# Scaling only one half of the query features, with a new hand-kept order of all operations

## The chip, the cores and the metric

The kernel runs on one core of a Trainium2 chip. The metric is the time on the device in microseconds (us), the median of several runs; the profile is of one execution. TensorE (PE in the profile) multiplies matrices, VectorE (DVE), ScalarE (ACT) and GpSimd (POOL) work element by element, and SyncE (SP) issues transfers. Every engine takes its own instructions strictly in order and waits for the others by semaphores.

## The reference

Two layers, each a linear attention followed by a gated feed-forward part, with a residual around both. There are 2048 tokens of 512 numbers, 32 heads of 16, and a feed-forward width of 1376.

```python
pq = einsum("bhsd,hdf->bhsf", q, w_phi);  pk = the same of k
phi_q = concat([softmax(pq), softmax(-pq)], -1);  phi_k = the same of pk
kv = einsum("bhsf,bhsd->bhfd", phi_k, v);  z = sum of phi_k over the tokens
o = (phi_q @ kv) / (phi_q @ z + 1e-6);  attention = o @ wo
# feed-forward: gate = x @ W_gate; h = relu(gate) * (x @ W_up); h @ W_down
x = x + attention(layernorm(x)); x = x + feed_forward(layernorm(x))   # twice
```

Both layers use the same weights. A softmax runs over the 16 numbers of one head.

## The kernel before, in words

The tokens are 16 tiles of 128 rows, kept in `X`. `fold` multiplies w_phi into the query and key weights once at the start, so that one projection gives `pq` or `pk` of a tile: w_phi is spread to block-diagonal form (`Wblk`, line 409), the weight blocks are transposed (`wT`) and multiplied with it (line 448), and copied to `Wk2` and `Wq2` (operations named `W2`). For the key weights the transposition is on TensorE (line 440), for the query weights by a transposing load on SP (line 435).

For every tile of a layer, `norm_A` computes the normalisation (statistics at line 477 and 478 on VectorE, logarithm and root at 485 and 487 on ScalarE, scaling at 495 on VectorE) and a transposition `xnTA`, by TensorE (line 466) for the first tiles, else by SP. `Keys` then does the key projection (line 535), exp(p) and exp(-p) (538, ScalarE) into the two halves of `ek`, the value projection (541) with its copy `vext` (425 on ScalarE or 426 on VectorE), the 64 sums over 16 numbers (546, VectorE), their reciprocal by logarithm and exponential (555, 558, ScalarE), two 512-wide multiplications by it (`halves`, line 509, VectorE or GpSimd), and the product with the values, summed up over all tiles (570). When all 16 tiles of a layer are in, `build` makes `R` of it (582, 587).

`query` does the same for queries: projection at 597, exponentials at 600, sums `sq` at 603, logarithm and exponential at 606 and 608, the two wide multiplications (line 509 again, named `phq`), and a transposition `fq` by SP (611). `attend` multiplies `fq` with `R` (622), divides (629 to 636), transposes (`oT`) and projects with wo (645), and adds to `X` (649). `mlp` centres (665), transposes (`xnTB`), squares (671 or 673), computes gate and up (722, and 698 for the last 96 columns), the product `hT` (726 to 739), and the down projection (762) with its sum into `X` (769). Feed-forward blocks are of 1, 1, 2, 4, 4, 2, 2 tiles in the first layer and 1, 1, 2, 4, 4, 2, 1, 1 in the second. The first gate matmul of the first block needs the whole of `R`, and so the keys and values of all 16 tiles.

Nothing is scheduled at run time. The 1880 operations are made in a fixed list, and four constants say the rest: `ORDER` is the order in which they are emitted (so also the order on each engine), `PLACE` has a digit for each operation that has two engines to choose from (1 takes the second), `SLOTS` names the buffer that each takes, and `IDLE` counts filler matmuls on zeros ahead of each of the first TensorE operations; eight more (`warm`, line 419) run while the first loads are under way. The four constants were computed beforehand by a planner with a model of the engines' costs; the costs at each `op(...)` are its inputs and have no effect on the chip.

Of the kernel before, what the change touches and what calls it, by code (L numbers as in the profile page):

```python
# [8 lines left out]
P = 128  # L9
D = 512  # L10
H = 32
DH = 16
F = 1376
NB = D // P
# [4 lines left out]
HB = 8  # L19
NG = 2 * NB  # L20
# [92 lines left out]
def dve(n, rate=1, more=66):  # L113
    t = n / rate / 0.96 + more
    return t, t + 98
# [27 lines left out]
class K:  # L143
# [9 lines left out]
    "0101110100000000001100000100110001000011010001111000000011001101010101001001001000101001111111011010"  # L153
    "1011110000000100000001001101000000000111011001011111010111000101001100000101111101001100001101010100"
    "1111111110101010010001000011000100000000101100101010100001001100011100010000110011001101000110111001"
    "010110010110111001110100110100000"
)
SLOTS = (
    "0001425210034050000151131234202310332121143404550125d3104c02302b3020a12113g533004002394131703202e141"
    "5i022124504f013k03583226105214413624335a011h100b033c05053623122j214910170400020501131002000245011020"  # L160
    "2500001142021002010100203200101143020002012105002004314023104g13300215112012320410311e34110200400450"
    "10205113120513d5100i42221240121321402422031200151030231042100142131004133610104f33242541002510104203"
    "51101520500512052130201550414201515300804024k2232c4020121152143124212004023502a533344112050010024104"
    "02024213011055002220j4203h05133317362b222f1506242i013a114023391638231c343e352k221d014g10011500020514"
    "0010124302000012011021450000121302100024010021050012201000011011521101530431102000005112025421011101"
    "0213125200125020013101050032154203115143114220221100253415210511200211401013403005210402213013222420"
    "500210300512431510432512113015114024105320310110512400202"
)
IDLE = (
    0, 0, 0, 0, 0, 0, 0, 0, 0, 0, 2, 0, 4, 0, 0, 0, 0, 0, 0, 0, 0,  # L170
# [108 lines left out]
def kernel(  # L279
# [11 lines left out]
    def new(name, shape, dt=BF16):  # L291
        return sb.tile([P] + shape, dt, name=name)
# [586 lines left out]
```

## Time and profile before

| | |
|---|---|
| median of three runs | 377.24 us (377.06 to 377.68) |
| profiled execution, span from first to last instruction | 375.3 us |
| TensorE busy | 364.6 us, 97% |
| VectorE, ScalarE, GpSimd busy | 285.1, 209.7, 93.5 us |
| granted TensorE clock | 1.000 |

The page gives no other time of the profiled execution than its span; the median lies 1.9 us above it. Busy times count an instruction from its start to its end; matmuls are pipelined, so a row of four that follow each other every 0.216 us is shown as 1.03 us long. In the lines of the profile a PE, DVE, ACT or POOL stands ahead of the line of the code, the operation, what it writes and reads, and how many instructions were merged.

### The profile page before, as it was taken

To read this page: it belongs to the slowest core of one execution; us is meant where nothing else is said; L and a number is where in the kernel's file an instruction comes from. 1 tells how busy PE (TensorE), PEld (TensorE's weight loads), DVE (VectorE), ACT (ScalarE), POOL (GpSimd) and SP (SyncE) were. 2 spreads that over 40 slices of the span, in tenths; PEclk is the share of its full clock that TensorE was granted. 3 is DMA by queue.
4 is the path that set the end of the run, shared out by engine and by line. 5 is a ranking of instruction groups with operands and counts; after the bars stand their busy time and mean duration, and the time that the engine had idled before them with its cause. 6 is when DMAs were issued, how large, how long until landed. Compare 5 with 4: busy or idle time off the path is not lost.

```text
span 375.3 us, 7459 instructions
## 1 busy us (share of the span) xinstructions
PE 364.6 (97%) x2793; PEld 216.6 (58%) x2833; DVE 285.1 (76%) x596; ACT 209.7 (56%) x553; POOL 93.5 (25%) x91
## 2 busy tenths in 40 slices
PE   8989997999999999999999999999999999999996
PEld 4534454868554554466476555587745444558585
DVE  6999999999998673685767999999994755543322
ACT  6989999746464532265155499973425323414031
POOL 0377984341010102001004269774000000000000
PEclk9999999999999999999999999999999999999999
DMA  8858844769814221012020102968664120211110
GB/s 256 191 139 175 312 58 85 123 113 132 164 36 84 47 53 31 11 25 56 9 56 2 29 2 57 141 93 142 143 132 85 31 56 2 56 29 51 42 51 30
DMA packets 93444, 31.21 MB, mean 83 GB/s; under 512 B 85248, under 2 KB 92384, under 8 KB 93408
## 3 DMA queue, kind: packets, MB, share of 16 engines
q1 hardware_dynamic: 92992, 30.34, 39.5%
q8 instruction: 22, 0.36, 0.4%
q10 hardware_dynamic: 416, 0.39, 0.3%
q14 instruction: 14, 0.11, 0.1%
HBM read 7.91 MB, written 2.10 MB: 27 GB/s over the span
## 4 chain that ended last, share of the span: by engine, by line
PE 90%; ACT 6%; DVE 1%; POOL 1%; issue 1%; DVEq 0%; another core or an unknown queue 0%
PE b L722 37%; PE b L762 20%; PE b L645 7%; PE b L541 6%; PE b L535 6%; PE b L597 6%; PE b L698 3%; PE q L622 2%; PE q L570 2%; ACT ek L600 1%; POOL ek L509 1%; ACT ek L538 1%; PE q L419 1%; DVE sq L603 1%; ACT hT L425 1%
## 5 line engine op out<-in xcount | busy, mean ns | idle before, releaser
L722 PE MATMUL b<-xnTB,wgu 128*128 128x128 bf16 (+2 forms) x1200 | 149.6, 279 | 0.0
L722 PEld LDWEIGHTS <-wgu 128*128 128x128 bf16 x1200 | 97.1, 98 | 43.6
L509 POOL TENSOR_TENSOR ek<-ek,sk 128x512 bf16<-128x512 bf16 x47 | 51.0, 1109 | 135.5 <-ACT sk L558 108.2
L726 ACT ACTIVATE gu<-b 128x512 bf16<-128x512 f32 (+1 forms) x83 | 47.8, 580 | 64.9 <-PE b L722 64.6
L762 PE MATMUL b<-wd,hT 128*128 128x512 bf16 (+2 forms) x350 | 81.3, 372 | 0.7
L762 PEld LDWEIGHTS <-hT 128*128 128x128 bf16 (+1 forms) x363 | 34.6, 98 | 35.9 <-DVE hT L739 0.2
L509 POOL TENSOR_TENSOR ek<-ek,sq 128x512 bf16<-128x512 bf16 x38 | 42.0, 1127 | 32.6 <-ACT sq L608 18.0
L739 DVE TENSOR_TENSOR hT<-gu,b 128x512 bf16<-128x512 bf16 (+1 forms) x44 | 29.6, 676 | 18.5 <-PE b L722 16.9
L546 DVE TENSOR_REDUCE sk<-ek 128x64 f32<-128x1024 bf16 x32 | 38.7, 1210 | 5.3 <-ACT ek L538 5.2
L538 ACT ACTIVATE ek<-b 128x512 bf16<-128x512 f32 x64 | 35.9, 598 | 9.2 <-PE b L535 8.0
L603 DVE TENSOR_REDUCE sq<-ek 128x64 f32<-128x1024 bf16 x32 | 38.2, 1207 | 0.3 <-POOL ek L509 0.3
L600 ACT ACTIVATE ek<-b 128x512 bf16<-128x512 f32 x64 | 36.1, 623 | 0.6 <-PE b L597 0.5
L730 DVE TENSOR_TENSOR hT<-gu 128x512 bf16<-128x512 bf16 (+1 forms) x39 | 16.7, 429 | 22.5 <-ACT gu L741 22.3
L769 DVE SCALAR_TENSOR_TENSOR X<-b,rsB,X 128x512 bf16<-128x512 f32 (+1 forms) x33 | 23.2, 726 | 13.5 <-PE b L762 13.4
L645 PE MATMUL b<-wo,oT 128*128 128x512 bf16 x118 | 31.2, 379 | 1.2 <-ACT oT L425 0.7
L535 PE MATMUL b<-Wk,xnTA 128*128 128x512 bf16 x122 | 31.4, 379 | 0.3
L541 PE MATMUL b<-wv,xnTA 128*128 128x512 bf16 x124 | 31.0, 379 | 0.4 <-ACT xnTA L425 0.2
L597 PE MATMUL b<-Wq,xnTA 128*128 128x512 bf16 x121 | 30.5, 379 | 0.3
L741 ACT CAST gu<-b 128x512 bf16<-128x512 f32 (+1 forms) x39 | 21.7, 558 | 15.0 <-PE b L722 14.6
L649 DVE SCALAR_TENSOR_TENSOR X<-b,X 128x512 bf16<-128x512 f32 x32 | 21.8, 682 | 3.5 <-PE b L645 3.4
L636 DVE TENSOR_TENSOR o<-q,rd 128x512 bf16<-128x512 f32 x32 | 21.9, 685 | 0.8 <-ACT rd L633 0.6
L477 DVE BATCH_NORM_STATS2 bstA<-X 128x6 f32<-128x512 bf16 x32 | 21.0, 681 | 1.9 <-DMA X<-in_A_x_dram 1.8
(71 smaller groups left out, 349.1 us busy)
## 6 DMA issues: line engine op xcount, KB each, us to landing
out_dram<-X SPq DMA_DIRECT2D x15, 128.0 KB, 1.7
X<-in_A_x_dram SPq DMA_DIRECT2D x6, 256.0 KB, 4.8
wgu<-in_B_W_gate_dram SPq DMA_DIRECT2D x4, 344.0 KB, 4.0
wgu<-in_B_W_up_dram SPq DMA_DIRECT2D x4, 344.0 KB, 3.6
wd<-in_B_W_down_dram SPq DMA_DIRECT2D x5, 256.0 KB, 3.6
wv<-in_A_wqkv_dram SPq DMA_DIRECT2D x2, 256.0 KB, 4.3
wo<-in_A_wo_dram SPq DMA_DIRECT2D x4, 128.0 KB, 3.2
fq<-ek SPq DMA_TRANSPOSE x32, 3.3
```

Of the source, the lines that this page charges most:

```text
L509: e.tensor_tensor(out=out().rearrange("p g s (h f) -> p (g s h) f", f=DH)[:, lo:lo + n], in0=ek.t[:].rearrange("p g s (h f) -> p (g s h) f ...
L535: k = op("PE", mm(4, 512), due, lambda: [nc.tensor.matmul(kp.t[:], lhsT=xnTA[c][:, i, b, :], rhs=Wk2[:, b, :], start=(b == 0), stop=(b == ...
L538: e = [op("ACT", act(512), due, lambda s=s: nc.scalar.activation(out=ek.t[:, :, s, :], in_=kp.t[:].rearrange("p (g e) -> p g e", e=GQ), fu ...
L541: v = op("PE", mm(4, 512), due_v, lambda: [nc.tensor.matmul(vp.t[:], lhsT=xnTA[c][:, i, b, :], rhs=wv[:, b, :], start=(b == 0), stop=(b == ...
L546: a = op("DVE", SUM16, due, lambda: nc.vector.tensor_reduce(out=sk.t[:, row, :], in_=ek.t[:].rearrange("p g s (h f) -> p (g s h) f", f=DH) ...
L597: q = op("PE", mm(4, 512), due, lambda: [nc.tensor.matmul(qp.t[:], lhsT=xnTA[c][:, i, b, :], rhs=Wq2[:, b, :], start=(b == 0), stop=(b == ...
L600: e = [op("ACT", act(512), due, lambda s=s: nc.scalar.activation(out=ek.t[:, :, s, :], in_=qp.t[:].rearrange("p (g e) -> p g e", e=GQ), fu ...
L603: a = op("DVE", SUM16, due, lambda: nc.vector.tensor_reduce(out=sq.t[:], in_=ek.t[:].rearrange("p g s (h f) -> p (g s h) f", f=DH), axis=A ...
L645: a = op("PE", mm(4, 512), due + 3, lambda j=j, yp=yp: [nc.tensor.matmul(yp.t[:], lhsT=oT.t[:, j, b, :], rhs=wo[:, b, :], start=(b == 0), ...
L722: nc.tensor.matmul(ps.t[:, q * W:(q + 1) * W].rearrange("p (i t) -> p i t", t=P), lhsT=wgu[:, s, b, g * P:(g + 1) * P], rhs=xT.t[:, 0:n, b ...
L726: nc.scalar.activation(out=gu.t[:, 0, 0:cols], in_=gp.t[:, 0:cols], func=AF.Relu)
L762: nc.tensor.matmul(yp.t[:, 0:c1 - c0], lhsT=h.t[:m, f * W + i * P:f * W + (i + 1) * P], rhs=wd[:m, f, c0:c1], start=(f == 0), stop=(f == N ...
```

## The change

For queries, numerator and denominator of the attention both carry the factor by which a row of a head's features is scaled. The change divides both halves by the sum of exp(-p): exp(-p) stays as it is, and exp(p) is multiplied by the ratio of the sum of exp(-p) to the sum of exp(p). Logarithm and exponential run over the 32 sums of exp(p) only; a new multiplication of 32 numbers makes the ratio (in the place of the first wide one of the list), and one 512-wide multiplication is left. w_phi is centred over its last index ahead of being spread, by two small instructions, which doesn't change a softmax. Keys are computed as before. The numbers in `ORDER`, `SLOTS` and `PLACE` are all new, and the count of operations stays 1880; the placement of the choices changes so:

| operation | before | after |
|---|---|---|
| query multiplications, 512 wide | 38 POOL, 26 DVE | 24 POOL, 8 DVE |
| query ratio, 32 numbers | none | 20 POOL, 12 DVE |
| key multiplications, 512 wide | 47 POOL, 17 DVE | 43 POOL, 21 DVE |
| value copies | 19 ACT, 13 DVE | 25 ACT, 7 DVE |
| folded-weight copies | 6 ACT, 2 DVE | 8 ACT |
| copies of the up projection, else a direct product | 39 ACT, 44 DVE | 36 ACT, 47 DVE |

```diff
 IDLE = (
-    0, 0, 0, 0, 0, 0, 0, 0, 0, 0, 2, 0, 4, 0, 0, 0, 0, 0, 0, 0, 0,
+    0, 0, 0, 1, 0, 0, 0, 0, 0, 0, 1, 0, 1, 0,
...
-    c_blk = op("DVE", dve(512), 20, lambda: nc.vector.tensor_tensor(
...
+    def blocks():
+        nc.vector.tensor_reduce(out=cmean[:], in_=wf[:], axis=AX.X, op=Alu.add)
+        nc.vector.scalar_tensor_tensor(out=wf[:], in0=cmean[:].unsqueeze(2).to_broadcast([P, NB, DH]),
+                                       scalar=-1.0 / DH, in1=wf[:], op0=Alu.mult, op1=Alu.add)
+        nc.vector.tensor_tensor(
+            out=Wblk[:].rearrange("p b (j f) -> p b j f", f=DH),
+            in0=wf[:].unsqueeze(2).to_broadcast([P, NB, HB, DH]),
+            in1=Mf[:].unsqueeze(1).unsqueeze(3).to_broadcast([P, NB, HB, DH]), op=Alu.mult)
...
+        pos, neg = (lambda: sq.t[:].rearrange("p (g s h) -> p g s h", s=2, h=HG)[:, :, 0, :],
+                    lambda: sq.t[:].rearrange("p (g s h) -> p g s h", s=2, h=HG)[:, :, 1, :])
         a = op("ACT", RLN[0], due, lambda: nc.scalar.activation(
-            out=sq.t[:], in_=sq.t[:], func=AF.Ln, scale=1.0), [a], (), [sq], name="lnq")
+            out=pos(), in_=pos(), func=AF.Ln, scale=1.0), [a], (), [sq], name="lnq")
         a = op("ACT", REXP[0], due, lambda: nc.scalar.activation(
-            out=sq.t[:], in_=sq.t[:], func=AF.Exp, scale=-1.0), [a], (), [sq], name="rq")
-        a = halves("phq", ek, lambda: ek.t[:], lambda lo, n: sq.t[:, lo:lo + n], PHI["POOL"], due, [a], [], [ek, sq])
+            out=pos(), in_=pos(), func=AF.Exp, scale=-1.0), [a], (), [sq], name="rq")
+
+        def ratio(e):
+            e.tensor_tensor(out=pos(), in0=pos(), in1=neg(), op=Alu.mult)
+
+        def scale(e):
+            v = ek.t[:, :, 0, :].rearrange("p g (h f) -> p g h f", f=DH)
+            e.tensor_tensor(out=v, in0=v, in1=pos().unsqueeze(3).to_broadcast([P, NG, HG, DH]), op=Alu.mult)
+        a = op("POOL", (212, 253), due, lambda: ratio(nc.gpsimd), [a], [], [ek, sq], name="rat", port=3,
+               alt=("DVE", DVE0, lambda: ratio(nc.vector), 1))
+        a = op("POOL", (1016, 1058), due, lambda: scale(nc.gpsimd), [a], [], [ek, sq], name="phq", port=3,
+               alt=("DVE", dve(512), lambda: scale(nc.vector), 1))
```

Of the new order the prediction speaks of these places (names as in the code, with the number of the tile or block; `load2` is the first half of the key weight, `load1` the second, `load3` is w_phi, `load4` and `load5` the value weight, `load0` and `load6` on the tiles of x):

```
SP before:  load2 load3 load4 load5 load6 load7 load8 load9 load10 ... load14 wT4
SP after:   load3 load2 load6 load7 load8 load9 load13 wT4 load5 load11 load4 load14 wT6
ACT before: load0 load1 tbl ln0 rstd0 wT0 wT3 wT1 wT2 W23 xnTA0 W22 W21 vext0
ACT after:  load0 tbl load1 ln0 rstd0 wT0 wT1 ln1 W20 rstd1 wT3 wT2 xnTA0 W21 W23 W22
DVE before: hr0 hr0 zero eps ones ... masks Mg stats0 aggr0 xnA0 Wblk W20 stats1
DVE after:  ones eps hr0 masks zero ones ones hr0 stats0 ones aggr0 Wblk stats1 ones aggr1 xnA0
PE before:  warm turn0 turn1 turn3 xnTA0 turn2 fold0 fold3 fold1 fold2 V0 K0 xnTA3 xnTA2 xnTA1 V3 K1
PE after:   warm turn0 turn1 fold0 turn3 turn2 xnTA0 fold1 fold3 fold2 fold4 xnTA1 K0 K1 xnTA3 V0 xnTA2
```

More of the change, by code (lines that the diff above doesn't have):

```diff
@@ L163 @@
[L163 to L167, printed above, removed]
+    "0011432021055021001401501045313321124221352412451013e0315g31303b0305c12201i012432332391030654220f321"
@@ L311 @@
     Wblk = new("Wblk", [NB, P])
+    cmean = new("cmean", [NB], F32)
     R = new("R", [NG, GE])
@@ L408 @@
     c_m = op("DVE", (230, 330), 10, masks, [c_id], name="masks")
[L409 to L412 removed]
+    def blocks():
[6 more added lines that the diff above has]
+            in1=Mf[:].unsqueeze(1).unsqueeze(3).to_broadcast([P, NB, HB, DH]), op=Alu.mult)
+    c_blk = op("DVE", (900, 1000), 20, blocks, [c_m, l_wf], name="Wblk", port=True)
     c_mg = op("DVE", DVE0, 15000, lambda: nc.vector.tensor_tensor(
```

25 lines of the change are left out of this document (13 added, 12 removed), and 183 rows, old and new, of the table ORDER.

## The prediction

> **What bounds the kernel now.** I read the page's first part and its chain of waits first, for the engine that ends last, then the busy time by windows, for the stage that has slack, then the timeline of the start and of the stage just ahead of the first feed-forward matmul.
>
> ```profile
> span 375.3 us, 7459 instructions
> ...
> PE 364.6 (97%) x2793; PEld 216.6 (58%) x2833; DVE 285.1 (76%) x596; ACT 209.7 (56%) x553; POOL 93.5 (25%) x91
> ...
> PE 90%; ACT 6%; DVE 1%; POOL 1%; issue 1%; DVEq 0%; another core or an unknown queue 0%
> ```
>
> TensorE is 90% of the chain that ended last; VectorE is far from full as an average. The averages hide the stage, so I cut the span:
>
> ```profile
> core 0: us, PE busy (x) PEld busy (x) DVE busy (x) ACT busy (x) POOL busy (x), PEclk, DMA share, GB/s
> 0.00:10.00 10.00, 8.30 (x53) 4.22 (x55) 6.27 (x24) 6.42 (x13) 0.70 (x6) 1.00 0.83 263
> 10.00:25.00 15.00, 13.11 (x100) 6.61 (x99) 14.86 (x31) 14.88 (x47) 8.30 (x8) 1.00 0.74 172
> 25.00:40.00 15.00, 14.88 (x92) 7.32 (x95) 14.93 (x27) 13.60 (x40) 11.12 (x10) 1.00 0.82 193
> 40.00:50.00 10.00, 9.89 (x80) 5.24 (x81) 9.99 (x10) 10.00 (x32) 10.00 (x11) 1.00 0.53 196
> 50.00:60.00 10.00, 9.77 (x80) 5.01 (x80) 10.00 (x15) 9.68 (x27) 6.74 (x6) 1.00 0.59 82
> 60.00:64.30 4.30, 2.59 (x33) 1.52 (x32) 4.26 (x7) 4.23 (x16) 2.12 (x2) 1.00 0.62 120
> 64.30:80.00 15.70, 15.54 (x219) 12.88 (x220) 15.70 (x35) 10.42 (x34) 5.70 (x5) 1.00 0.76 123
> ...
> 220.00:240.00 20.00, 19.84 (x155) 10.26 (x155) 19.49 (x23) 19.67 (x58) 19.83 (x19) 1.00 0.43 66
> ...
> 340.00:360.00 20.00, 19.90 (x172) 14.37 (x172) 6.06 (x11) 6.46 (x12) 0.00 (x0) 1.00 0.16 45
> ```
>
> From 64.3 us on TensorE stands idle for next to nothing: 0.16 us in the 20 at the layer boundary, where the other three engines are just as full, and 0.10 in the 20 near the end. Nothing that makes VectorE or GpSimd lighter there can shorten the span. Before 64.3 us, from 10 us on, VectorE is full (0.37 us idle in 54) and ScalarE nearly, while TensorE has holes. The first feed-forward matmul needs all keys and values, hence VectorE's sums. **So the change pays only by what it takes off the front, up to the first gate matmul:**
>
> ```profile
> 1.01 0.27 DVE L396 MEMSET zero<- 128x256 uint32 x1
> ...
> 1.34 3.60 PE L419 MATMUL q<-zero 128*128 128x512 bf16 x8 [1.34 <-DVE zero L396]
> 1.34 0.28 DVE L405 TENSOR_REDUCE Mf<-ident 128x8 f32<-128x128 bf16 x1
> ...
> 1.67 1.28 ACT L373 ACT_TABLE_LOAD   x1 [1.67 <-PEq L863]
> ...
> 4.72 0.90 PE L440 MATMUL b<-ident,hT 128*128 128x128 bf16 x12
> ...
> 5.22 2.05 ACT L425 CAST hT<-b 128x512 bf16<-128x512 f32 x4 [0.16 <-PE b L440]
> ...
> 7.19 1.87 DVE L477 BATCH_NORM_STATS2 bstA<-X 128x6 f32<-128x512 bf16 x3
> ...
> 9.18 1.03 PE L535 MATMUL b<-Wk,xnTA 128*128 128x512 bf16 x4
> ...
> 10.04 1.03 PE L419 MATMUL q<-zero 128*128 128x512 bf16 x4
> ...
> 34.04 1.89 PE L535 MATMUL b<-Wk,xnTA 128*128 128x512 bf16 x8
> ...
> 42.32 0.67 PE L570 MATMUL q<-vext,ek 128*128 128x65 bf16 x16
> ...
> 56.68 1.56 ACT L600 ACTIVATE ek<-b 128x512 bf16<-128x512 f32 x3
> ...
> 64.25 1.95 PE L722 MATMUL b<-xnTB,wgu 128*128 128x128 bf16 x32
> ```
>
> The columns are start, length, engine, line, operation and count. The first key projection runs at 9.18, the first gate matmul (call it G0) at 64.25, and everything behind G0 takes 375.3 - 64.25 = 311.0 us. The profiled execution's span is 375.3; the median of the runs is 377.24, so 1.9 us lie around the span, and I carry them along.
>
> TensorE's own need between the two marks: four 512-wide matmuls start to start in 0.863 us (a row of eight lasts 1.89, one of four 1.03), a group of eight K'V matmuls in about 0.25 (sixteen in 0.67, less the tail of 0.17), a transposition of four 128-wide ones in some 0.225 (twelve in 0.90, tail included). By the code's list the old order has, between the end of K0 at 10.04 and G0, 47 projections (40.5), 19 small groups (4.8), ten transpositions and folds (2.25) and one filler group (0.86): 48.4 us in 54.2. TensorE stalls 5.8 us there, and that is the sum the change can win from.
>
> **The change part by part.** The operation list keeps its length, so order and placement can be read number by number. Prices for the other engines, from the groups of instructions by form (count, then busy us and mean ns of one, then the idle time before them):
>
> ```profile
> L509 DVE TENSOR_TENSOR ek<-ek,sq 128x512 bf16<-128x512 bf16 x26 | 19.1, 744 | 0.0
> ...
> L509 DVE TENSOR_TENSOR ek<-ek,sk 128x512 bf16<-128x512 bf16 x17 | 11.8, 708 | 1.2 <-ACT sk L558 1.2
> ...
> L426 DVE CAST vext<-b 128x512 bf16<-128x512 f32 x13 | 8.8, 680 | 1.2 <-PE b L541 1.2
> ...
> L426 DVE CAST Wk<-b 128x512 bf16<-128x512 f32 x1 | 0.7, 692 | 0.5 <-PE b L448 0.5
> ...
> L413 DVE TENSOR_TENSOR Mg<-Mf 128x4 f32<-128x4 f32 x1 | 0.2, 161 | 0.0
> ...
> L671 ACT ACTIVATE wasteA<-X 128x512 bf16<-128x512 bf16 x21 | 13.2, 627 | 14.5 <-DVE X L649 13.2 <-issue 1.1
> ...
> L608 ACT ACTIVATE sq<-sq 128x64 f32<-128x64 f32 x32 | 8.7, 275 | 0.2
> ...
> L509 POOL TENSOR_TENSOR ek<-ek,sk 128x512 bf16<-128x512 bf16 x47 | 51.0, 1109 | 135.5 <-ACT sk L558 108.2 <-DVE ek L509 24.8 <-DVE X L769 2.4
> L509 POOL TENSOR_TENSOR ek<-ek,sq 128x512 bf16<-128x512 bf16 x38 | 42.0, 1127 | 32.6 <-ACT sq L608 18.0 <-PE b L722 6.3 <-DVE lnB L677 4.9
> ```
>
> *Query scaling.* Each of 32 query tiles had two 512-wide multiplies (38 on GpSimd, 26 on VectorE); it now has one, and one multiply of 32 numbers. The new placement puts 24 wide and 20 small ones on GpSimd, 8 and 12 on VectorE. No row shows the small one. On VectorE the nearest is the 128x4 multiply, 0.16 us; on GpSimd it lies between that and a wide one, 1.1. I take 0.16 and 0.3, near the small row, for it has a sixteenth of the elements. A query's path on GpSimd goes from two passes in turn (2.2 us) to 1.4; at the upper bound it stays at 2.2. Over the kernel GpSimd loses 18 wide passes of 1.1 (four key passes leave it too) and VectorE 14 of 0.7. Most of that lies beside a full TensorE and is worth nothing; it only hides better. What the new model could win by keeping VectorE and GpSimd out of each other's way is small: VectorE's 43 wide passes are 0.744 and 0.708 on the mean against 0.68 for its plain copies, 2.1 us in all, over the whole span. The logarithm and reciprocal handle 32 columns where they had 64; there is no row for 32, so between nothing and half of 0.275 each; I take nothing.
>
> *VectorE ahead of the first centring (line 665), by the list.* Query passes go from 4 to 1 (3 x 0.744 = 2.2), value copies from 5 to 3 (1.4), folded-weight copies from 2 to none (1.4); one key pass more (0.7), and the centring of w_phi adds two small instructions on 64 elements (0.16 each as the least; at most a 512-wide one, 0.68 each; I take 0.3 for both). Sum: -4.0; instructions in a row overlap a little (three statistics in 1.87 are 0.62 each against 0.68), so **-3.7 us**. Centring delays the block weights, but the first fold waits longer for the transposed weight on ScalarE, which covers it; uncovered it costs its 0.3.
>
> *ScalarE ahead of the evacuation that G0 waits for.* Seven exponentials of queries now come behind it (7 x 0.52, three in 1.56), as do two logarithms, two reciprocals (4 x 0.27) and one square (0.63); ahead come two folded-weight and two value copies (4 x 0.51, four in 2.05). Sum: -3.64 - 1.1 - 0.6 + 2.05 = **-3.3 us**.
>
> *The start is later.* The zeros for the eight warm-up matmuls now stand behind the mask sums on VectorE: 1.34 + 0.28 + 0.27 = 1.9, so warm-up begins some 0.6 later than at 1.34, and the first weight transposition at 5.35 instead of 4.72 (the eight take 3.38). On ScalarE the table load (1.28) now stands ahead of the second half of wk, which is therefore asked for 1.3 later; w_phi goes ahead of the first half on SP, both wv halves behind x tiles and a transposing load, so V0 moves behind K1. ScalarE starts its nine wide evacuations up to the last quarter of the folded K weight at 5.35 + 0.5 = 5.85 (the 0.5 as from 4.72 to 5.22); all four quarters are now its own. Nine times 0.51 plus two small activations (0.275 each) end at 10.99: K0 at about **11.0 instead of 9.18**. Between nothing lost and the 1.8, I take it in full.
>
> **The sum.** G0 by each engine: TensorE 11.9 plus its 48 projections, 19 small groups and eight transpositions (41.4 + 4.75 + 1.8 = 47.95): not before 59.85. VectorE: 64.25 - 3.7 + 0.3 = 60.85. ScalarE: 64.25 - 3.3 + 0.6 (its later first evacuation) = 61.55. The latest holds, and three engines that are nearly level wait for each other more; for that I add 0.7, an estimate (old TensorE stalls of 5.8, of which it still has 2.4): G0 at 62.25, 2.0 us sooner. TensorE has next to no slack behind, so the 311.0 us stay: span 373.25, **time 375.2 us**. Late next is ScalarE's queue of exponentials.
>
> **Rivals.** *The late start isn't absorbed.* If TensorE's stalls behind K0 stay at 5.8, because they come from the serial steps (exponential, sum, logarithm, scaling) and not from full queues, G0 is 11.9 + 47.95 + 5.8 = 65.65, 1.4 late: 378.6; were the late half of wk to hold the fold up 1.3 more, 379.9. It decides from 4.4 us of stalls on. For it: K0 moves back 1.8 by plain queue order. Against: VectorE is never idle from 10 us on, so less of its work must show.
>
> *New waits behind G0.* The whole order is new. A stall where TensorE now has none would eat the gain: one at the layer boundary of as much as the old front's worst (60 to 64.3: 1.7 us) gives 376.9, which is the case of no change. Against: GpSimd and VectorE have less to do there, and 11 instead of 10 of layer 1's query projections come ahead of its first attention group.
>
> *All engines overlap as their lists allow.* G0 at TensorE's 59.85: 4.4 sooner, 372.8; with ScalarE's copies moved as counted this needs its queue to be lighter than 61.55 says.
>
> *A cold array.* Between warm-up and K0 TensorE has 2.9 us of small groups and 0.65 of filler (one group each in three places, where the old order had two and four in two) for 5.65 us. The eight warm-up matmuls took 0.42 each, the later filler 0.22 (a row of four lasts 1.03 with its tail). If the array went back to the slow pace there, it would lose half of another 3.4 us: 1.7, which lifts TensorE's bound from 59.85 to 61.55, level with ScalarE's, and costs perhaps 0.7 more waiting: 375.9. By the Trainium skill, TensorE: Matmul & The Clock Gate, Part 1, the clock halves after an idle window of about 3.4 us and needs one busy window to come back, which speaks against thinning out the filler. In the trace the projections right behind the holes at 8 to 11 us still ran at 0.22 each, so it hasn't happened at holes of that size.
>
> **Chances.** Forecast and its neighbours (G0 0.8 to 3 us sooner) 0.42; the lists overlap fully 0.05; cold array, faster still 0.04; late start not absorbed 0.27; new waits behind G0 0.22, of which half about cancel the gain and half go beyond to the slow side. A measurement of this kernel tells some 0.2% (0.75 us) from no change. That gives faster 0.51, same 0.11, slower 0.38. The forecast's own range is 374.2 to 376.4; the whole range, from the full overlap's 372.8 up to the late start's worst, 379.9, leaves out larger stalls behind G0.
>
> **What would show it.** Right: K0 near 11.0, G0 between 61.5 and 63, 24 wide and 20 small multiplies of queries on GpSimd, VectorE still full from 10 to 60, and 311 us from G0 to the end. Wrong: K0 later than 12, G0 at 64.3 or behind, TensorE waits for GpSimd or VectorE of over 1 us behind G0, or a tail behind G0 that differs from 311 by more than 1 us.

## The result: 0.28% faster, about half of what was forecast

| | before | after |
|---|---|---|
| time, median of six runs | 377.54 us (377.06 to 377.70) | 376.48 us (375.87 to 376.53) |
| ratio, 95% interval | | 0.9972 [0.9963, 0.9982] |
| span of the profiled execution | 375.28 us | 374.65 us |
| first key projection K0 | 9.18 | 10.18 (forecast 11.0) |
| last group of products of keys and values ends | 55.13 | 55.40 |
| first gate matmul G0 | 64.25 | 62.74 (forecast 62.25) |
| from G0 to the end | 311.03 | 311.91 (forecast 311.0) |

In the runs of before and after the time lies 1.7 to 1.9 us above the span (in f and l, below, 2.1 to 2.2). The profiled execution of before was the fastest of its runs, so spans alone show 0.63 us of the 1.06 that the medians show; where the text below compares single points of two profiles, it compares one execution of each.

The page of after, with the parts that were shown of before (span; busy time of the engines; the chain by engine):

```profile
span 374.7 us, 7403 instructions
...
PE 363.8 (97%) x2784; PEld 216.1 (58%) x2830; DVE 275.9 (74%) x587; ACT 204.3 (55%) x561; POOL 80.4 (21%) x93
...
PE 89%; issue 1%; ACT 0%; DVE 0%; DVEq 0%
```

VectorE lost 9 us, ScalarE 5, GpSimd 13, TensorE 0.8 (three fillers fewer). Of some 28 us of work that went, 1 us came off the time. The same windows, now with the cut at the new G0:

```profile
0.00:10.00 10.00, 7.26 (x54) 3.91 (x56) 6.92 (x25) 5.58 (x13) 0.70 (x6) 1.00 0.83 239
10.00:25.00 15.00, 14.58 (x96) 7.19 (x96) 14.59 (x31) 15.00 (x45) 7.24 (x8) 1.00 0.99 216
25.00:40.00 15.00, 13.28 (x87) 6.46 (x88) 15.00 (x24) 12.82 (x40) 10.84 (x12) 1.00 0.80 180
...
50.00:60.00 10.00, 9.86 (x109) 5.71 (x110) 9.99 (x13) 9.40 (x30) 8.72 (x11) 1.00 0.49 106
60.00:62.80 2.80, 2.46 (x32) 1.42 (x31) 2.58 (x6) 2.31 (x8) 1.06 (x2) 1.00 1.08 179
62.80:80.00 17.20, 17.04 (x239) 13.68 (x239) 16.50 (x38) 12.75 (x44) 6.89 (x10) 1.00 0.82 151
220.00:240.00 20.00, 19.76 (x214) 11.55 (x216) 19.04 (x31) 14.99 (x41) 5.24 (x7) 1.00 0.08 15
```

TensorE gained from 10 to 25 us (14.58 busy instead of 13.11) and ahead of G0 (0.34 idle in 2.8 instead of 1.71 in 4.3), and lost from 25 to 40 us (13.28 instead of 14.88) while VectorE is full. These are the two places that the experiments are about.

**The place of the loss.** From the timeline of after, all engines, 26 to 32 us:

```profile
26.78 2.12 POOL L513 TENSOR_TENSOR ek<-ek,sk 128x512 bf16<-128x512 bf16 x2 [0.74 <-ACT sk L562]
26.84 2.21 DVE L499 TENSOR_SCALAR xn<-X,mvA,rsA 128x512 bf16<-128x512 bf16 x2
...
29.30 1.04 PE L539 MATMUL b<-Wk,xnTA 128*128 128x512 bf16 x4 [0.57 <-DMA xnTA<-xn]
...
29.97 0.29 ACT L489 ACTIVATE lnA<-mvA,eps 128x2 f32<-128x2 f32 x1 [2.15 <-DVE mvA L482]
...
31.38 1.02 PE L545 MATMUL b<-wv,xnTA 128*128 128x512 bf16 x4 [1.04 <-ACT ek L604]
```

Two normalisations on VectorE take 2.21 us where two others take 0.73 (30.96 us, alone). They begin 0.06 us behind two passes on GpSimd and end 0.15 us behind them: VectorE stands locked out, 1.16 and 1.14 us for an instruction of 0.41. A third one, at 20.55, took 1.13. The statistics behind them come late, ScalarE waits 2.15 us for these, and TensorE waits 0.57 and then 1.04 us. Before had none of these in its first 64 us. The Trainium skill, SBUF — State Buffer, section Who interferes with whom, says just this: such a scaling in its two-port form and a GpSimd instruction take the shared ports for the whole instruction, whoever starts first. The trace agrees, 1.16 beside 0.41 us.

**The place of the gain**, from the last products of keys and values (L570, L574) to G0. TensorE's timeline of before:

```profile
54.46 0.67 PE L570 MATMUL q<-vext,ek 128*128 128x65 bf16 x16
55.19 2.54 PE L597 MATMUL b<-Wq,xnTA 128*128 128x512 bf16 x11
57.56 0.42 PE L622 MATMUL q<-R,fq 128*128 128x68 bf16 x8
57.82 1.89 PE L597 MATMUL b<-Wq,xnTA 128*128 128x512 bf16 x8
59.88 0.40 PE L466 MATMUL b<-ident,o 128*128 128x128 bf16 x4 [0.17 <-DVE o L636]
60.95 1.04 PE L645 MATMUL b<-wo,oT 128*128 128x512 bf16 x4 [0.68 <-ACT oT L425]
...
63.18 0.40 PE L466 MATMUL b<-ident,xn 128*128 128x128 bf16 x4 [0.84 <-DVE xn L665]
```

and of after:

```profile
54.73 0.67 PE L574 MATMUL q<-vext,ek 128*128 128x65 bf16 x16
55.46 0.81 PE L601 MATMUL b<-Wq,xnTA 128*128 128x512 bf16 x3
56.30 0.42 PE L638 MATMUL q<-R,fq 128*128 128x68 bf16 x8
56.56 1.89 PE L601 MATMUL b<-Wq,xnTA 128*128 128x512 bf16 x8
58.28 0.39 PE L470 MATMUL b<-ident,o 128*128 128x128 bf16 x4
58.51 1.03 PE L601 MATMUL b<-Wq,xnTA 128*128 128x512 bf16 x4
...
60.49 1.02 PE L601 MATMUL b<-Wq,xnTA 128*128 128x512 bf16 x4
```

Before runs three query projections (11 of the 12 matmuls are recorded) ahead of the first attention group and two behind it; after runs one ahead and four behind, in the waits of the serial chain: attention group, division, transposition, output projection, residual, centring, gate. And on VectorE, between R and the first division (`o`), before has two wide query scalings, after none. From VectorE's timelines, before and then after:

```profile
57.79 1.43 DVE L509 TENSOR_TENSOR ek<-ek,sq 128x512 bf16<-128x512 bf16 x2
59.15 0.68 DVE L636 TENSOR_TENSOR o<-q,rd 128x512 bf16<-128x512 f32 x1
```

```profile
57.38 0.69 DVE L652 TENSOR_TENSOR o<-q,rd 128x512 bf16<-128x512 f32 x1
```

From the last product of keys and values to G0 it is 64.25 - 55.13 = 9.12 us before and 62.74 - 55.40 = 7.34 after: 1.78 us gained here, 0.27 lost ahead of it, 0.88 lost behind it.

### The profile page after: what moved, and what is told of

Read it like the earlier page. It is cut to its first block, busy times and chain, and to the rows that moved or that the text cites. A ratio compares the mean times of both kernels' runs of the same rounds, so it can differ in the third digit from the quotient of the medians.

```text
span 374.7 us, 7403 instructions
## 1 busy us (share of the span) xinstructions
PE 363.8 (97%) x2784; PEld 216.1 (58%) x2830; DVE 275.9 (74%) x587; ACT 204.3 (55%) x561; POOL 80.4 (21%) x93
## 4 chain that ended last, share of the span: by engine, by line
PE 89%; issue 1%; ACT 0%; DVE 0%; DVEq 0%
PE b L738 37%; PE b L778 20%; PE b L661 7%; PE b L601 6%; PE b L545 6%; PE b L539 5%; PE b L714 3%; PE q L638 2%; PE q L574 2%; PE b L470 1%; ACT ek L604 0%; DVE o L652 0%; DVE X L785 0%; DVEq L890 0%; ACT lnA L489 0%
## 5 line engine op out<-in xcount | busy, mean ns | idle before, releaser
L738 PE MATMUL b<-xnTB,wgu 128*128 128x128 bf16 (+2 forms) x1200 | 154.5, 279 | 0.2 <-ACT rd L649 0.2
L778 PE MATMUL b<-wd,hT 128*128 128x512 bf16 (+2 forms) x342 | 83.9, 372 | 0.9
L513 POOL TENSOR_TENSOR ek<-ek,sk 128x512 bf16<-128x512 bf16 x43 | 46.7, 1107 | 122.6 <-ACT sk L562 121.7
L755 DVE TENSOR_TENSOR hT<-gu,b 128x512 bf16<-128x512 bf16 (+1 forms) x47 | 30.8, 666 | 30.2 <-ACT gu L742 16.4
L604 ACT ACTIVATE ek<-b 128x512 bf16<-128x512 f32 x64 | 37.0, 606 | 6.9 <-PE b L601 6.7
L542 ACT ACTIVATE ek<-b 128x512 bf16<-128x512 f32 x64 | 36.8, 623 | 6.6 <-PE b L539 6.6
L757 ACT CAST gu<-b 128x512 bf16<-128x512 f32 (+1 forms) x36 | 20.5, 569 | 25.9 <-PE b L738 25.7
L539 PE MATMUL b<-Wk,xnTA 128*128 128x512 bf16 x122 | 32.2, 379 | 1.1 <-DMA xnTA<-xn 0.6
L545 PE MATMUL b<-wv,xnTA 128*128 128x512 bf16 x124 | 31.8, 379 | 1.3 <-ACT ek L604 1.0
L622 POOL TENSOR_TENSOR ek<-ek,sq 128x512 bf16<-128x512 bf16 x24 | 25.3, 1060 | 30.4 <-DVE rsB L701 14.3
L746 DVE TENSOR_TENSOR hT<-gu 128x512 bf16<-128x512 bf16 (+1 forms) x36 | 15.2, 424 | 10.1 <-ACT gu L757 10.0
```

The lines of the kernel that those rows point to most:

```text
L513: e.tensor_tensor(out=out().rearrange("p g s (h f) -> p (g s h) f", f=DH)[:, lo:lo + n], in0=ek.t[:].rearrange("p g s (h f) -> p (g s h) f ...
L539: k = op("PE", mm(4, 512), due, lambda: [nc.tensor.matmul(kp.t[:], lhsT=xnTA[c][:, i, b, :], rhs=Wk2[:, b, :], start=(b == 0), stop=(b == ...
L542: e = [op("ACT", act(512), due, lambda s=s: nc.scalar.activation(out=ek.t[:, :, s, :], in_=kp.t[:].rearrange("p (g e) -> p g e", e=GQ), fu ...
L545: v = op("PE", mm(4, 512), due_v, lambda: [nc.tensor.matmul(vp.t[:], lhsT=xnTA[c][:, i, b, :], rhs=wv[:, b, :], start=(b == 0), stop=(b == ...
L604: e = [op("ACT", act(512), due, lambda s=s: nc.scalar.activation(out=ek.t[:, :, s, :], in_=qp.t[:].rearrange("p (g e) -> p g e", e=GQ), fu ...
L738: nc.tensor.matmul(ps.t[:, q * W:(q + 1) * W].rearrange("p (i t) -> p i t", t=P), lhsT=wgu[:, s, b, g * P:(g + 1) * P], rhs=xT.t[:, 0:n, b ...
```

## The experiments

The theory at first was the prediction's: lighter queues on VectorE and ScalarE bring G0 forward. The rivals were that the order does it, or that locks, the start, or waits behind G0 decide the size. Ratios are to the kernel before on the same chip, five rounds each.

**Order and scaling apart.** Two kernels with one half of the change each.

```diff
 a_oldorder_newscale: code of after (scaling, centring), with before's ORDER, SLOTS and IDLE
+the ratio takes the place of a tile's first wide multiply; in 13 of layer 0's 16 tiles the wide one is on VectorE
 b_neworder_oldscale: ORDER, SLOTS and IDLE of after, with before's code of the scaling
```

> The new scaling and the centring with the old ORDER, SLOTS, PLACE and IDLE: in each query pair the first multiplication of the old order becomes the small ratio, the second the one wide scaling, on the engines that the old order gave to these places. Theory A (the front is bound by the engines' queues, the order has only to use what the scaling frees): four of the query passes ahead of the first centring are some 2 us of VectorE and now 2 small and 2 wide ones, so G0 comes 0.5 to 1.2 us sooner than at 64.25 and the time is 0.2 to 0.4% below the kernel before. Rival B (only the new order pays): no change from the kernel before, within 0.2%.

> The new ORDER, SLOTS, PLACE and IDLE with the old scaling of queries (two wide multiplications, the first in the place of the ratio) and without centring. Theory A: seven ratios ahead of the first gate matmul become wide passes of GpSimd, 0.8 us more each, but VectorE has the same work there, so G0 moves by less than 0.5 us from that of the changed kernel and the time lies between the two, 0.1 to 0.3% below the kernel before. Rival B (only the order pays): the same as the changed kernel, 0.28% below the kernel before. Rival C (the order needs the lighter GpSimd): slower than the kernel before by 0.3% or more.

| | last K'V ends | G0 | behind | median | ratio |
|---|---|---|---|---|---|
| a | 55.09 | 64.16 | 311.60 | 377.62 | 1.0013 [1.0005, 1.0022] |
| b | 57.79 | 65.49 | 318.13 | 385.25 | 1.0220 [1.0206, 1.0233] |

Neither half gains. The lighter scaling in the old order moves nothing; the new order with the old scaling loses 2.2%. The gain needs both.

**Locks.** c takes two of the three normalisations out of the way of GpSimd, h the third as well, d reads and writes every second number, in the hope that the instruction then leaves the shared ports alone.

```diff
 c_xn_first, VectorE:  -stats10 stats15 xnA6 xnA7   +xnA6 xnA7 stats10 stats15
 h_xn_all, VectorE:    c, and xnA9 directly behind xnA8
 d_step2:              -out=xn[:, j], in0=x        +out, in0 as "p (c s) -> p s c", s=2, for tiles 6, 7 and 9
```

> The changed kernel with one pair of statistics (tiles 10 and 15) moved behind the scaling of tiles 6 and 7 on VectorE, so that the scaling runs before GpSimd starts its two passes at 26.8 us. Lock theory: the scaling no longer waits out two GpSimd passes (2 x 0.73 us), TensorE's stalls at 29.3 (0.73) and 31.4 (1.21) shrink by 1 us or more, G0 comes 0.8 to 1.5 us sooner, and the time is 0.2 to 0.4% below the changed kernel. Rival (the transposing transfers on SP, queued behind weight loads, set these stalls): the scaling takes 0.41 us, the stalls stay, and the time is that of the changed kernel within 0.1%.

> The changed kernel with all three locked scalings moved ahead of GpSimd's passes: statistics of tiles 10 and 15 behind the scaling of tiles 6 and 7, and the scaling of tile 9 directly behind that of tile 8. Lock theory: no scaling in the first 64 us lasts over 0.6 us, and G0 comes another 0.2 to 0.7 us sooner than with two of them moved (61.42); time 0.2 to 0.4% below the changed kernel. Rival (the third lock is covered by other queues): G0 at 61.4 again, time as with two moved.

> The changed kernel, same order and engines; only the scaling of tiles 6, 7 and 9 of the first layer reads and writes every second element, then the rest. If that takes the instruction out of the mode in which it shares a port with GpSimd, each lasts some 0.6 to 0.65 us whatever GpSimd does, instead of 1.13 to 1.16 with a lock and 0.41 without. Lock theory: 0.5 us less in each of three places, TensorE's stalls at 29.3 and 31.4 shrink by 0.7 us or more, time 0.15 to 0.3% below the changed kernel. Rival (transfers): no change within 0.1%. Rival (the wait isn't the lock's): still over 1.1 us each.

c: G0 at 61.42, 1.32 us sooner than after; 375.71 us, 0.9963 [0.9951, 0.9975]. h: G0 61.73, 376.00 us, 0.9961 [0.9949, 0.9973], so the third lock had been covered. d: G0 63.14, 376.81 us, 0.9987 [0.9979, 0.9996]. TensorE's wait in c, and VectorE's normalisations in d:

```profile
30.06 1.02 PE L551 MATMUL b<-wv,xnTA 128*128 128x512 bf16 x4 [0.57 <-ACT ek L610]
```

```profile
20.69 1.30 DVE L500 TENSOR_SCALAR xn<-X,mvA,rsA 128x512 bf16<-128x512 bf16 x1
27.11 2.38 DVE L500 TENSOR_SCALAR xn<-X,mvA,rsA 128x512 bf16<-128x512 bf16 x2
```

In c the wait at 29.3 is gone, the other has halved, and the same value projection starts 1.32 us sooner (30.06 instead of 31.38), as G0 does: the locks cost after what the trace says, 1.3 us in its front. In time the ratios, each to before on the same chip, put it at some 0.3 us (0.9963 beside 0.9972), and their intervals overlap: what c gains over after at G0 is seen in the profile, what it gains in time is not clear of the noise. In d each of the three is still locked, so this way out fails here; the Trainium skill, VectorE: DVE Perf Modes, section What auto-detection actually checks, ties only the packed form to a step of one and not the use of both ports, and the 1.30 us agree.

**The start, and everything at once.** e brings the start back, m and g reorder more of VectorE's statistics and ScalarE's exponentials on top of c and h.

```diff
 e_start:        SP -load3 load2  +load2 load3;  VectorE: the zeros for the warm-up first
 g_all:          h and e; ScalarE: both exponentials of tile 2 ahead of ln9
 m_stats_first:  c; VectorE: stats15 stats14 aggr15 aggr14 ahead of stats10
```

> The changed kernel with the first half of the key weight asked for ahead of w_phi again, and the zeros for the warm-up matmuls ahead of the other fills on VectorE. Theory (a late start is a lasting loss, since ScalarE and TensorE are full behind it): first transposition 0.4 to 0.6 us earlier than at 5.57, G0 0.3 to 0.6 us earlier than at 62.74, time 0.1 to 0.15% below the changed kernel. Rival (the front absorbs it): the start moves and G0 does not, time the same within 0.1%.

> All three scalings moved, the start mended, and the two query exponentials of tile 2 put ahead of the logarithm that waits for the statistics of tiles 10 and 11 on ScalarE, so that the value projection that stalled at 31.4 gets its buffer. If the stalls are what sets G0 and each is on TensorE's path, they add up: the stall at 30 us falls from 0.73 to under 0.2, G0 at 60 to 60.8, time 0.4 to 0.6% below the changed kernel and 0.7 to 0.9% below the kernel before. Rival (the next queue takes over): G0 no earlier than 61, time no more than 0.35% below the changed kernel.

> The kernel with two scalings moved ahead of GpSimd's passes, and now the statistics of tiles 15 and 14 and their sums ahead of those of tiles 10 and 11 on VectorE, so that ScalarE's logarithm of that pair and the two query exponentials queued behind it run some 0.7 us sooner. Theory (what is left of the stall, 0.73 us at 30.1, is that wait): stall under 0.2, G0 0.4 to 0.7 us sooner than at 61.42, time 0.3 to 0.4% below the changed kernel. Rival (a new lock or the next queue takes it back, as in the kernel with all edits): G0 at 61.4 or later, and some scaling lasts over 1 us.

| | first transposition | K0 | G0 | median | ratio |
|---|---|---|---|---|---|
| after | 5.57 | 10.18 | 62.74 | 376.48 | 0.9972 |
| e | 4.36 | 10.17 | 62.79 | 376.87 | 0.9975 [0.9964, 0.9985] |
| g | 4.56 | 10.47 | 63.03 | 377.17 | 0.9998 [0.9987, 1.0008] |
| m | 5.44 | 10.06 | 64.58 | 377.41 | 0.9998 [0.9988, 1.0008] |

e starts 1.2 us sooner and gains nothing: K0 waits for the folded weight, whose later pieces wait for ScalarE's copies at the same time as in after (8.57 and 8.58 us). Part of the gain e gives back itself, for w_phi is loaded later and the first fold waits 1.18 us for it. That the start is off the path in every order is so not shown; this way of starting sooner brings nothing. g and m make new locks (normalisations of 1.10 and 1.14 us at 29.85 and 30.86 in g, 0.94 and 1.14 in m) and a TensorE wait of 1.14 and 2.07 us at 32.6: moving work away from one collision moved it into the next. The profiled execution of m also had a stretch of half TensorE clock from 33.5 us on (last section), so up to 1.7 us of its 64.58 may come from that; its nine executions without it took 377.08 us in the median, still no better than after.

**Layer 1, and the centring.** f gives layer 1's queries their two wide multiplies back; l leaves the centring out.

```diff
 f_l1_twice:  +if l == 0: (scaling of after) else: (both halves multiplied, as before)
 l_nocentre:  -tensor_reduce(cmean, wf)  -scalar_tensor_tensor(wf, cmean, -1/16, wf)
```

> The changed kernel with the old scaling (two wide multiplications, logarithm and exponential over 64 sums) for the queries of the second layer only. What the prediction said (behind G0 TensorE has no slack to lose, GpSimd's and VectorE's passes hide): time of the changed kernel within 0.2%. Rival, from the run with the new order and the old scaling in both layers (8 us over, some 5.9 of it in stalls behind 220 us): 1.2 to 1.7% slower than the changed kernel, with stalls of 4 to 6 us between 220 and 270 us, where wide passes on VectorE last up to 1.5 us because GpSimd's go first.

> The changed kernel without the centring of w_phi (its two small instructions are left out, so exp(-p) goes unscaled by what a centred p would give; the quotient is the same but for the small constant under it). Prediction: the two cost nothing, since the first fold waits longer for ScalarE; time of the changed kernel within 0.1%, first fold at 6.8 us as before. Rival (they are on the start's path): first fold and K0 0.3 to 0.4 us sooner; even so the start is absorbed and G0 stays within 0.2 us.

f: G0 62.92, behind it 317.41 us instead of 311.91, 382.16 us, 1.0126 [1.0111, 1.0141]. l: G0 62.78, 377.04 us, 0.9979 [0.9966, 0.9993]. The centring is covered. And f's 5.5 us lie at waits such as this one in TensorE's timeline:

```profile
253.34 1.05 PE L745 MATMUL b<-xnTB,wgu 128*128 128x128 bf16 x16 [1.62 <-DVE hT L762]
```

So the new order leaves VectorE and GpSimd so little room behind G0 that it lives on the lighter scaling there; the old order had room for two multiplies.

**Is it VectorE's load?** i and k take wide multiplies, and in k two value copies too, to the other engine in the old order.

```diff
 i_wide_pool:       a, the wide multiply of 13 layer-0 tiles: -VectorE  +GpSimd
 k_wide_pool_vext:  i, value copies of tiles 10 and 6: -ScalarE  +VectorE
```

> The old order with the new scaling once more, but in 13 of the first layer's 16 query tiles the one wide multiplication moves from VectorE to GpSimd and the small ratio the other way (in the first such kernel the wide one had stayed on VectorE, and VectorE was as full as before). Ahead of the first gate matmul VectorE loses four wide passes of 0.7 us and gains small ones: some 2 us. Theory (VectorE's queue bounds the front): G0 1 to 1.7 us sooner than at 64.16, time 0.25 to 0.45% below the kernel before. Rival (the waits at 59 to 64 us are steps of one chain that ScalarE's queue and the fixed places set): VectorE shows idle time there, G0 within 0.4 us of 64.2, time within 0.15% of the kernel before.

> The same, with the value copies of tiles 10 and 6 moved from ScalarE to VectorE as well. If ScalarE's queue bounds the front once VectorE has room, G0 comes another 0.5 to 1 us sooner than without this. If the chain's fixed steps set it: no change within 0.3 us. If VectorE still bounds it: 0.5 to 1 us later.

i: G0 65.44, 378.57 us, 1.0028 [1.0015, 1.0041]; k: 66.15, 378.34 us, 1.0030 [1.0019, 1.0041]. From 57 to 64 us VectorE is busy 6.07 us in i (6.82 in a), and G0 comes later: the feature transposition `fq` now waits for a GpSimd pass of 1.1 us, and TensorE for `fq` (0.67 us in i, 0.80 in k). The profiled executions of both had TensorE at half clock for some 3.4 us, from 63.6 us on in i and 64.3 in k, which puts an estimated 0.5 us into these G0; the waits for `fq` lie ahead of it, and the executions at full clock were slower than before too (medians of 378.43 us in i and 378.32 in k). A lighter VectorE is not the cause by itself.

**The place of the query projections.** o and q move them in the old order, with the old and the new scaling; n moves two back in after.

```diff
 o_before_q (before) and q_a_q (a), TensorE:
-Q7 Q15 Q10 erq0 Q14 Q9 oT0 proj0
+Q7 erq0 Q15 Q10 oT0 Q14 proj0 Q9      their exponentials on ScalarE behind them
 VectorE: one wide multiply of tile 2's features from ahead of R to behind it
 n_back (after), TensorE:  -Q7 erq0 Q9 Q15 oT0   +Q7 Q9 Q15 erq0 oT0
```

(The expectation of o names tile 5 for the wide multiply; the kernels move tile 2's.)

> The kernel before, with the old scaling. Only the order of some operations between the last key-value group and G0 is changed: the first attention group comes right behind one query projection, and the projections of tiles 15, 10, 14 and 9 come behind it, in the waits of the chain that leads to G0; their exponentials follow on ScalarE, and one wide scaling of tile 5 comes behind R on VectorE. Theory (place of the projections): the first attention group starts 1.0 to 1.5 us sooner than 57.56, G0 0.5 to 1.5 us sooner than 64.25, time 376.0 to 377.0, ratio to before 0.996 to 0.999. Rival (the order of the whole front): G0 within 0.3 us of 64.25, ratio 0.999 to 1.001. A second rival (the exponentials that were moved behind are then late for layer 1's and the block's later steps): G0 sooner, but more behind it, ratio 1.000 to 1.003.

> The old order with the new scaling and the centring (kernel a), with the same edit of the order. Theory (place of the projections): G0 0.5 to 1.5 us sooner than a's 64.16, ratio to before 0.997 to 0.999. If the lighter scaling is what lets the moved projections pay, this gains 0.3 us or more over the same edit with the old scaling. Rival (the order of the whole front): G0 within 0.3 us of a's 64.16, ratio 1.000 to 1.002.

> The kernel after, with the query projections of tiles 9 and 15 moved back ahead of the first attention group, and nothing else. Theory (place of the projections): the first attention group starts 1.5 to 1.8 us later than 56.30, G0 1.0 to 1.5 us later than 62.74, time 377.4 to 378.0, ratio to before 0.9995 to 1.001: the gain is gone. Rival (the order of the whole front): the chain behind it gets shorter by as much, G0 within 0.3 us of 62.74, ratio 0.996 to 0.998.

| | last K'V ends | first attention group | G0 | last K'V to G0 | median | ratio |
|---|---|---|---|---|---|---|
| before | 55.13 | 57.56 | 64.25 | 9.12 | 377.54 | 1 |
| o | 55.01 | 56.44 | 66.51 | 11.50 | 380.91 | 1.0095 [1.0080, 1.0110] |
| q | 55.35 | 56.23 | 65.88 | 10.53 | 379.09 | 1.0056 [1.0035, 1.0078] |
| after | 55.40 | 56.30 | 62.74 | 7.34 | 376.48 | 0.9972 [0.9963, 0.9982] |
| n | 57.07 | 59.50 | 65.66 | 8.59 | 377.91 | 1.0017 [1.0006, 1.0028] |

In the new order the place is worth all of the gain: two projections moved back cost 1.25 us in the stage and 1.43 us in the median, as the theory said. The K'V of n ends 1.67 us later than that of after, and that has another cause. n's instructions up to there are those of after, its normalisations are locked as long (2.22 us for two), and the value projection that after starts at 31.38 us starts at 31.40 in n. The 1.67 us are lost behind it: in this one execution of n, its slowest of twelve, TensorE ran at half clock from 32.6 to 36.0 us (last section). The stage from the last K'V to G0 lies behind that.

In the old order the theory missed, on the other side: the first attention group does come 1.1 us sooner in o, but the division stays at 59.41, behind the sum and the wide scalings, and TensorE, with its projections spent elsewhere, waits 1.56 us for it. In q, too, G0 is later than before. Half clock doesn't explain these two: in their profiled executions it begins only at 65.7 us in o, where it can hold an estimated 0.4 us of the 66.51, and at 65.8 in q. It is in all four executions of o and in two of six of q, whose other four took 378.48 us and more, above the 377.49 of before on that chip.

**What is queued at the division.** s puts two wide scalings into that place in after; u takes them out of it in q, and ScalarE's exponentials from ahead of the two logarithms and reciprocals.

```diff
 s_two_dve (after), wide multiply of tiles 2 and 4:  -GpSimd  +VectorE, both between sq5 and the first division (o)
 u_chain (q), the same two:  -VectorE  +GpSimd
 u_chain (q), ScalarE:  exponentials of tiles 10, 15, 9: -ahead of rden0, rden1  +behind them
```

> The kernel after, with the wide scalings of query tiles 2 and 4 on VectorE instead of GpSimd, in the place where the old order has two: between the building of R and the first division (1.3 us of VectorE). Nothing else is changed; GpSimd gets 2.1 us free. Theory (VectorE's queue in the chain to G0 is the other half of the gain): first division 1.0 to 1.3 us later than 57.38, G0 0.7 to 1.3 us later than 62.74, time 377.1 to 377.8, ratio to before 0.999 to 1.001. Rival (only the place of the query projections counts): G0 within 0.3 us of 62.74, ratio 0.996 to 0.998.

> Kernel q (old order with the lighter scaling and the query projections moved into the chain), with the wide scalings of tiles 2 and 4 on GpSimd instead of between R and the first division on VectorE, and with the exponentials of tiles 9, 10 and 15 on ScalarE moved behind the logarithms and reciprocals of the first two divisions. Theory (the chain from R to G0, kept free on all three engines, is the gain, and the rest of the new order is not needed): first division near 57.8 to 58.4 instead of 59.15, G0 62.6 to 63.6 instead of q's 65.88, ratio to before 0.995 to 0.999. Rival (the order of the whole front is needed): G0 at 64 or later, ratio 1.000 to 1.006.

s: from the last K'V (55.93) to G0 (64.25) 8.32 us, 377.53 us, 1.0004 [0.9995, 1.0013]: the gain is gone. Its timelines, VectorE and then TensorE:

```profile
57.85 1.28 DVE L628 TENSOR_TENSOR ek<-ek,sq 128x512 bf16<-128x512 bf16 x2
59.05 0.68 DVE L658 TENSOR_TENSOR o<-q,rd 128x512 bf16<-128x512 f32 x1
```

```profile
59.78 0.40 PE L476 MATMUL b<-ident,o 128*128 128x128 bf16 x4 [0.79 <-DVE o L658]
```

1.28 us of VectorE in this one place cost 0.98 us of the stage and 1.05 us of the median. The 1.25 us of n and the 0.98 of s are together more than the 1.78 gained in the stage, so they are not two shares of it: each of the two places undoes most of the gain by itself, and the gain needs both. u: last K'V (55.23) to G0 (65.81) 10.58 us, 380.31 us, 1.0077 [1.0063, 1.0091], a miss. VectorE's next sum there waits for the pass that went to GpSimd, and one wide scaling still stands ahead of the division:

```profile
56.85 1.22 DVE L613 TENSOR_REDUCE sq<-ek 128x64 f32<-128x1024 bf16 x1 [0.80 <-POOL ek L628]
57.99 0.94 DVE L628 TENSOR_TENSOR ek<-ek,sq 128x512 bf16<-128x512 bf16 x1
58.85 0.68 DVE L658 TENSOR_TENSOR o<-q,rd 128x512 bf16<-128x512 f32 x1
```

and ahead of G0 TensorE waits for a copy on ScalarE:

```profile
65.81 1.50 PE L744 MATMUL b<-xnTB,wgu 128*128 128x128 bf16 x14 [1.07 <-ACT xnTB L435]
```

So the division is only 0.3 us sooner than in before (58.85 instead of 59.15; expected were 57.8 to 58.4), and u leaves the place half filled: it is no clean test of an empty one. (Its half clock begins at 66.0 us, behind G0.) Each repair of the old order that I tried ran into the next queue; so the rest of the new order, which feeds these queues in time, is probably part of the gain. I have not shown that, nor which part.

## Why the prediction was right in sign and wrong in size

Two steps of the sum failed. "The 311.0 us stay" was read from the old order and taken over to the new one: the tail behind G0 took 311.91 us, 0.9 more. And VectorE and GpSimd in each other's way were called small and got no term for the new order: the locks cost G0 1.3 us. Of the 2.0 us forecast, 1.06 came.

**Right.** The change pays only ahead of G0, and there it paid: 1.51 of the 2.0 us forecast. The late start was absorbed: G0 came sooner in spite of it, and starting sooner (e) brought nothing, so that rival (0.27) fell. Centring is covered (0.18 and 0.22 us, l). VectorE is still full from 25 to 60 us (from 10 to 25 it has 0.41 idle). 24 wide and 20 small query multiplies run on GpSimd:

```profile
L499 DVE TENSOR_SCALAR xn<-X,mvA,rsA 128x512 bf16<-128x512 bf16 x32 | 14.8, 481 | 2.7 <-ACT rsA L491 2.6
L618 POOL TENSOR_TENSOR sq<-sq 128x32 f32<-128x32 f32 x20 | 8.1, 408 | 36.9 <-ACT sq L614 30.9 <-DVE xn L499 5.9
L614 ACT ACTIVATE sq<-sq 128x32 f32<-128x32 f32 x32 | 7.0, 235 | 0.3
L618 DVE TENSOR_TENSOR sq<-sq 128x32 f32<-128x32 f32 x12 | 2.3, 190 | 1.1 <-ACT sq L614 1.1
```

(Groups of after: line, engine, operation, count, then busy us and mean ns.) The small multiply is 0.41 us on GpSimd and 0.19 on VectorE; I took 0.3 and 0.16.

**The error, in terms of the sum.** 376.48 - 375.2 = 1.28 us: G0 0.49 later than forecast, what lies behind it 0.91 longer, 0.12 less around the span.

- *"311.0 us stay"* failed. Read from the old order, where TensorE had no idle time behind G0, it was taken over to an order that had not been seen. After waits there in small places, the largest 0.34 us at 82.1 for a reciprocal, then 0.19 at 234.6, 0.16 at 258.4 and 0.13 at 71.05 (counted by the starts of its matmuls): 0.82 us in all, where such waits come to 0.14 in before. A longer tail is no accident of one execution: it took 311.9 to 312.5 us in c, d, e, g, h, l, m, n and s, which have the order and the scaling of after but for the moves named above, and 311.6 in a, with the new scaling in the old order. "What lies beside a full TensorE is worth nothing" was false for the new order as well: in layer 1 alone the lighter scaling is worth 5.5 us (f). The rival of new waits named the mechanism, and half of its size.
- *The lock* was priced by a mean over the wide multiplies and called small. Its victims were others, the normalisations, whose mean went from 0.421 to 0.481 us; three instructions in the front cost VectorE 2.2 us more, two of them on the path, and G0 1.3 us (c). That is more than the whole error of G0. It fits the rest: TensorE's stalls between K0 and G0 were to be 2.4 us and came to some 2.9 by the starts of its matmuls, of which 1.9 lie at the two waits of the lock (1.6 of them shown as idle).
- *VectorE's and ScalarE's queues, as sums* (-3.7, -3.3). A sum over a queue doesn't say what a piece is worth. The same 1.3 us of VectorE are worth nothing in most places (a, i) and 1.0 us between R and the first division (s). That the forecast of G0 came out within 0.5 us was luck in good part: the sums were the wrong measure, and they came near because the new order took the passes out of that one place and put the query projections into the waits. The prediction counted these passes, but not where they stand, and it didn't look at the projections.
- *K0 at 11.0* was late by 0.8. From the start of after (PE, then ACT with its queue):

```profile
1.96 3.59 PE L423 MATMUL q<-zero 128*128 128x512 bf16 x8 [1.96 <-DVE zero L394]
5.57 0.82 PE L444 MATMUL b<-ident,hT 128*128 128x128 bf16 x8
...
10.18 0.59 PE L539 MATMUL b<-Wk,xnTA 128*128 128x512 bf16 x2
```

```profile
1.19 1.28 ACT L371 ACT_TABLE_LOAD   x1 [1.19 <-PEq L879]
1.22 0.47 ACTq L346 DMA_DIRECT2D hT<-in_A_wqkv_dram  x1
```

The second half of the key weight is issued at 1.22, beside the table load and not 1.3 us behind it. And K0 starts on the quarters of the weight that are ready; I had it wait for the last of them.

**The other rivals.** The full overlap did not come. The cold array did not come in after, whose granted clock is 1.00 in all windows, but it came in some executions of eight of the experiments (below). Where its cost can be read from runs, in m, it was about 1.3 us, more than the whole change brings.

## What to carry to other kernels

Price a piece of work by its place: here 1.28 us of VectorE ahead of the first step of a serial chain cost 0.98 us of the stage (s), and a lighter VectorE without a new order gained nothing (a). Look at such a place for the waiting engine's cover (independent matmuls kept back for the waits) and for what stands ahead of the chain's own instructions on each engine. Before taking over "the rest stays as it is" from an old schedule to a new one, ask what room the new one has left; and when two engines share ports, look at which instructions will overlap, not at the mean over all.

Taking two normalisations out of GpSimd's way (c) has the lowest ratio found, 375.71 us, 0.9963 [0.9951, 0.9975], and h equals it; their intervals overlap that of after, so that they are faster than it is not shown.

## What the hardware showed beside that

The clock fell to half for about 3.4 us after waits far shorter than that, in some executions of eight kernels: by the mean granted clock (0.995 or 0.996 instead of some 1.00) 1 of 12 of g, 3 of 12 of i, 2 of 11 of k, 3 of 12 of m, 1 of 12 of n, 4 of 4 of o, 2 of 6 of q and 4 of 6 of u. Of all but g, the profiled execution is one of these. Windows of n:

```profile
28.00:32.00 4.00, 2.13 (x17) 1.03 (x16) 4.00 (x11) 2.01 (x7) 1.35 (x2) 1.00 0.46 110
32.00:36.00 4.00, 4.00 (x19) 1.70 (x18) 4.00 (x7) 3.27 (x11) 3.26 (x4) 0.57 0.76 183
```

and TensorE's wait between them, with what ran ahead of it and behind:

```profile
28.51 1.02 PE L545 MATMUL b<-Wk,xnTA 128*128 128x512 bf16 x4
31.40 1.02 PE L551 MATMUL b<-wv,xnTA 128*128 128x512 bf16 x4 [1.87 <-ACT ek L610]
32.35 1.69 PE L545 MATMUL b<-Wk,xnTA 128*128 128x512 bf16 x4
```

TensorE was idle for 1.87 us in one piece, and the clock stands at 0.57 over the next four: 0.43 x 4 / 0.5 = 3.4 us of it at half clock. (After has 1.61 us of idle time there in two pieces, 0.57 at 29.30 and 1.04 at 31.38, and kept its clock.) The loss of clock is 0.43 x 4 = 1.7 us of matmul time; in m the runs at a mean clock of 0.995 took 378.18 to 378.48 us, the others 377.08 in the median, so about 1.3 us reach the time. s, with a wait of 1.59 us in the same place, kept its clock. The Trainium skill, TensorE: Matmul & The Clock Gate, section HAM oscillation, gives as its abstract rule that idle gaps over some 3.4 us are to be avoided. The runs show half clock behind gaps of about half that length, and that the same kernel has it in one execution and not in another (n in one of twelve).
